# q and k turned in chunks of 128 tokens, two to a transposing DMA

## The chip, the cores and the metric

The kernel runs on one core of a Trainium2 chip. The metric is the device time of one execution in microseconds (us), the median over several runs. An engine of the core is named as in the profile: PE is TensorE (PEld its weight loads), DVE is VectorE, ACT is ScalarE, POOL is GpSimd, SP is SyncE, which computes nothing here and only issues DMAs. Each engine works through its own list of instructions in order; semaphores tie the lists together.

## What is computed

Sliding-window attention over 8 batches of 8 heads, 576 tokens and head size 64, and then a feed-forward part on the 8 x 576 = 4608 rows of 512 numbers that come out:

```
scores = (q @ k.T) / 8, kept where 0 <= row - col < 64, else -1e9
attn   = softmax(scores)              # per batch and head
x      = (attn @ v), heads side by side  -> [4608, 512]
h      = x @ w_in                     # [512, 2048]
out    = (h * cos(h)) @ w_out         # [2048, 512] -> float32 [4608, 512]
```

## The kernel before

**Blocks and groups.** A batch has NU = 9 blocks of 64 tokens. Because of the window, the queries of block j see only the keys of blocks j-1 and j, so a unit of attention is a 64 x 128 piece of scores. Four units make a group (`groups`), which goes through a chain of steps: scores on TensorE (s_ps), row maximum with mask on DVE (`g_max`), exponential and row sum on ACT (`g_exp`), reciprocal on DVE (`g_inv`), scaling to bf16 on POOL (`g_norm`, tile w), and the transpose of w into wT (`g_trans`), which for most groups is a DMA transpose issued by SP (L395). TensorE then multiplies wT by v (`values`, o_ps, L411), and DVE or ACT copies the result to xT.

**Token tiles.** The second part works on tiles of MT = 512 rows, n_mt = 9 of them. For a tile mt the loop at the end of the kernel first makes 16 blocks of h (`first` and `skewed`, h_ps, L479, 64 matmuls), lets ACT take the sine of each with a phase of pi/2 (L709) and DVE multiply (L712), and then makes the output rows (out_ps, L723, 64 matmuls, or in the last two tiles the seven products of `fast_second`). The 576 tokens of a batch don't fill whole tiles: tile mt takes the last mt blocks of batch mt - 1 and the first 8 - mt of batch mt.

**What sets the order.** Nothing is scheduled by the framework: each engine runs its instructions in the order in which the program writes them. The start (batches 0 and 1, tile 0, the loads of batch 2) is a list written out by hand, `FIRST`: `Lq2.3` in it is the load of chunk 3 of q of batch 2, `Lk2.0` of chunk 0 of k. From tile 1 on, a small planner orders the rest: `at(time, fn, ...)` puts a step down for a time, a tile being T = 32 units long, and `pump(time)`, called between pieces of the two matmul loops, writes out all steps that are due. So a step's time says between which matmuls it stands, and on SP and POOL it stands behind all that was written for them before. For batch b, t0 = T(b - 1) is the start of tile b - 1's loop, and the scores of batch b stand there as two bursts (`burst_scores`, L310), at t0 + 14.6 and t0 + 20.2 or a little later, the first with blocks 0 to 3.

**How q and k get there.** Scores need q and k with the head dimension on the partitions, that is, turned. For batches 2 to 7:

- `load_chunk` (L180): POOL issues a DMA that loads one chunk of NP = 96 tokens, all eight heads, of q or k, from float32 to bf16, into 96 partitions. Six chunks (NC) make a batch. Two buffers per name (pool `ld`).
- `turn_k` (L260): SP issues a DMA transpose per chunk into the tile kT, laid out [128, 4 pairs of heads, 576 tokens]; six per batch, written at t0 - 6 for b > 2.
- `turn_q` (L248): the same for q, into qT, for the first chunks only: `TURNED = {4: 2, 5: 2, 6: 2, 7: 6}`, so two chunks of batches 4 to 6, all six of batch 7, none of batches 2 and 3. Written at t0 - T + 23.4 (24.3 for b = 4, and 26.4 for chunks 2 to 5).
- `tr_q` with `transposed` (L223): the other chunks of q are turned by TensorE, per pair of heads one transpose a chunk into the PSUM tile tq_ps, and `put_q` lets DVE copy that to qT (L125). They stand in the loop over h of tile b - 1, at t0 + 1, 4.5, 8 and 11.5 (2, 5.3, 8.6 and 11.9 for b = 2), ahead of the first burst of the same batch.

The order that this gives SP around a tile's end is: the first four wT of a batch (t0 + 18.4 to 22.7), the turns of q of the next batch, two more wT, the turns of k of the next batch, the last wT, two stores of output (L488). `values` for tile mt is written at T mt - 1.01, so the first wT of batch mt are wanted there. `keys`, `burst_scores` and `g_scores` are the readers of qT and kT; they take 64 tokens of q and the 64 or 128 tokens of k of a unit as slices.

Of the kernel before, what the change touches and what calls it, by code (L numbers as in the profile page):

```python
# [10 lines left out]
def _safe_warn(msg, *a, **kw):  # L11
# [19 lines left out]
PAIRS = 4  # L31
# [8 lines left out]
TURNED = {4: 2, 5: 2, 6: 2, 7: 6}  # L40
# [29 lines left out]
def kernel(  # L70
# [28 lines left out]
    qsets = [const.tile([128, PAIRS, S], BF16, name=f"qT{i}") for i in range(2)]  # L99
# [76 lines left out]
    def load_chunk(name, b, c):  # L176
        if (name, b) not in st:
            st[name, b] = rows_tile(name)[0:NP].rearrange("p (c x) -> p c x", c=NC)
        src = {"q": q, "k": k}[name][b, :, c * NP:c * NP + NP]
        nc.gpsimd.dma_start(out=st[name, b][:, c].rearrange("p (h d) -> p h d", h=H),  # L180
                            in_=src.rearrange("h p d -> p h d"))
# [25 lines left out]
    def transposed(name, b, p):  # L207
# [13 lines left out]
        else:  # L221
            for c in range(TURNED.get(b, 0) if name == "q" else 0, NC):
                nc.tensor.transpose(t_ps[:, NP * c:NP * c + NP], of[:, c, 128 * p:128 * p + 128], ident[:NP, :NP])  # L223
# [3 lines left out]
    def in_order(t_ps, to, b, p):  # L227
        c = RC if b == p == 0 else NC
        return (t_ps.rearrange("d (c p) -> d p c", c=c), to.rearrange("d (p c) -> d p c", c=c)) if b < 2 else (t_ps, to)
# [4 lines left out]
    def put_q(b, p, engine=None):  # L234
        if b > 1:
            lo = TURNED.get(b, 0) * NP
            copy(engine, qsets[b % 2][:, p, lo:], st.pop(("tq", b, p))[:, lo:])
            return
        of, to = in_order(st.pop(("tq", b, p)), qsets[b][:, p], b, p)
# [7 lines left out]
    def turn_q(b, c):  # L247
        nc.sync.dma_start(out=qsets[b % 2][:, :, c * NP:c * NP + NP], in_=st["q", b][:, c], transpose=True)  # L248
# [4 lines left out]
    def k_tile(b):  # L253
        if ("kA", b) not in st:
            st["kA", b] = ka = att.tile([128, PAIRS, S], BF16, tag="kT", name="kT", bufs=2)
            st.update({("kT", b, p): ka[:, p] for p in range(PAIRS)})
        return st["kA", b]

    def turn_k(b, c):
        nc.sync.dma_start(out=k_tile(b)[:, :, c * NP:c * NP + NP], in_=st["k", b][:, c], transpose=True)  # L260

    def put_k(b, p, engine="a"):
        kt = k_tile(b)[:, p]
# [27 lines left out]
    def keys(b, p, j):  # L291
        lo, chunks = max(64 * j - 64, 0), 2 if j else 1
        rhs = st["kT", b, p][:, lo:lo + 64 * chunks].rearrange("d (a t) -> d a t", a=chunks)
# [469 lines left out]
```

## Time and profile before

| what | value |
|---|---|
| time, median of 3 runs (lowest to highest) | 303.11 us (302.81 to 303.87) |
| span of the profiled execution, first to last instruction | 301.0 us |
| busy: PE, DVE, ACT, POOL | 294.0, 234.7, 232.2, 210.3 us |
| mean granted TensorE clock | 1.000 |
| DMA packets, bytes | 159627, 41.45 MB |
| transposing DMAs issued by SP: wT, kT, qT | 60, 36, 12 |
| loads of q and k chunks issued by POOL | 36 and 36, 96 KB each |
| TensorE transposes of q, batches 2 to 6 (L223) | 96 |

The profile shows one execution, and of it the span alone; the runs' median lies 2.1 us above it. A row of a group reads: line, engine, operation, output tile <- input tiles, shape and count, then busy time and the mean of one in ns, then the idle time of the engine just before. In a table of stretches, "31.51, 31.48 (x289)" is the length of the stretch, then the busy time of the first engine in it with its number of instructions. SP's instructions are DMA issues; their duration is how long SP was held, and the landing is counted from the start of the issue to the arrival of the data.

### The profile page before, as it was taken

How to read it: one execution, taken by the hardware profiler on the slowest of the kernel's cores; microseconds unless marked ns; L12 is line 12 of the kernel's file. 1: busy time of each engine (PE TensorE's matmuls, PEld its weight loads, DVE VectorE, ACT ScalarE, POOL GpSimd, SP SyncE). 2: the span in 40 equal slices, each digit the busy share in tenths (PEclk: the TensorE clock that was granted, in tenths of full speed). 3: DMA queues.
4: the chain of work that ended last, by engine and by line, in shares of the span. 5: the costliest groups of instructions: out<-in, count | busy, mean ns of one | idle time of the engine just before them, and what ended most of it. 6: DMA issues, size and time to landing. Idle time of an engine off the chain costs nothing.

```text
span 301.0 us, 8375 instructions
## 1 busy us (share of the span) xinstructions
PE 294.0 (98%) x2863; PEld 162.5 (54%) x2863; DVE 234.7 (78%) x916; ACT 232.2 (77%) x781; POOL 210.3 (70%) x238
## 2 busy tenths in 40 slices
PE   8888999999999999999999999999999999999996
PEld 3667854644455445444454445444544454785485
DVE  4997888898887886788678876887588658985794
ACT  5997699877987699769986998699978997304610
POOL 8999568995899579995999599969997860000000
PEclk9999999999999999999999999999999999999999
DMA  7999999999999994999999999999999745003013
GB/s 146 179 206 195 198 186 138 99 154 156 219 124 112 230 119 75 115 152 188 174 108 145 165 216 115 126 152 205 134 101 119 212 86 174 2 3 139 1 37 105
DMA packets 159627, 41.45 MB, mean 138 GB/s; under 512 B 146976, under 2 KB 155232, under 8 KB 159584
## 3 DMA queue, kind: packets, MB, share of 16 engines
q0 software_dynamic: 101088, 18.06, 79.6%
q1 hardware_dynamic: 58352, 22.79, 42.3%
q8 instruction: 22, 0.36, 0.5%
q14 instruction: 21, 0.17, 0.2%
q10 hardware_dynamic: 144, 0.07, 0.1%
HBM read 36.70 MB, written 9.44 MB: 153 GB/s over the span
## 4 chain that ended last, share of the span: by engine, by line
PE 90%; DMA 4%; POOL 4%; DVE 1%; issue 0%; POOLq 0%
PE h_ps L479 37%; PE out_ps L723 28%; PE out_ps L566 8%; PE out_ps L462 5%; DMA w_in<-in_moe_w_in_dram 4%; PE h_ps L443 4%; PE s_ps L310 3%; PE o_ps L411 3%; PE tq_ps L223 1%; POOL v L186 1%; POOL q L164 1%; POOL k L164 1%; PE s_ps L332 1%; POOL w_in L202 0%; DVE xT L125 0%; PE tw_ps L392 0%
## 5 line engine op out<-in xcount | busy, mean ns | idle before, releaser
L479 PE MATMUL h_ps<-xT,w_in 128*128 128x512 bf16 x512 | 115.1, 379 | 0.2
L712 DVE TENSOR_TENSOR gT<-h_ps,sin 128x512 bf16<-128x512 f32 x128 | 85.2, 688 | 25.8 <-ACT sin L709 25.2
L709 ACT ACTIVATE sin<-h_ps 128x512 f32<-128x512 f32 x128 | 73.8, 598 | 37.0 <-PE h_ps L479 36.7
L359 ACT ACTIVATE e<-s,negm 128x128 f32<-128x128 f32 (+1 forms) x256 | 97.1, 382 | 1.7 <-POOL v L125 1.0
L723 PE MATMUL out_ps<-w_out,gT 128*128 128x512 bf16 x384 | 85.3, 379 | 0.0
L376 POOL TENSOR_TENSOR w<-e,rden 128x512 bf16<-128x512 f32 (+1 forms) x68 | 69.0, 1032 | 21.8 <-DVE rden L369 15.9
L479 PEld LDWEIGHTS <-w_in 128*128 128x128 bf16 x512 | 48.9, 98 | 54.5
L723 PEld LDWEIGHTS <-gT 128*128 128x128 bf16 x384 | 36.5, 98 | 43.1
L347 DVE CUSTOM_DVE_ANT_0 s<-s_ps,mask 128x128 f32<-128x128 f32 (+1 forms) x256 | 56.0, 277 | 1.8 <-PE s_ps L332 1.5
L359 ACT ACTIVATION_READ_ACCUMULATOR e<-s,negm 128x1 f32 x256 | 48.1, 188 | 0.0
L186 POOL DMA_DIRECT2D v<-in_v_dram x40 | 34.1, 870 | 0.1
L180 POOL DMA_DIRECT2D q<-in_q_dram x36 | 28.7, 801 | 7.7 <-DMA k<-in_k_dram 3.0
L180 POOL DMA_DIRECT2D k<-in_k_dram x36 | 28.7, 799 | 1.5 <-DVE gT L712 0.7
L369 DVE RECIPROCAL rden<-den 128x4 f32<-128x4 f32 (+1 forms) x73 | 12.2, 167 | 18.7 <-ACT e L359 18.3
L125 POOL COPY v<-v 64x1536 bf16<-64x1536 bf16 (+3 forms) x16 | 22.9, 1433 | 0.4
L347 DVE DVE_READ_ACCUMULATOR2_ANT negm<- 128x1 f32 x256 | 21.3, 83 | 0.0
L125 DVE CAST xT<-o_ps 128x512 bf16<-128x512 f32 x24 | 15.6, 679 | 4.6 <-PE o_ps L411 4.4
L443 PE MATMUL h_ps<-xT,w_in 128*128 128x256 bf16 x128 | 14.6, 273 | 0.4 <-DMA w_in<-in_moe_w_in_dram 0.4
L462 PE MATMUL out_ps<-w_out,gT 128*128 128x512 bf16 x64 | 14.8, 380 | 0.0
L443 PEld LDWEIGHTS <-w_in 128*128 128x128 bf16 x128 | 12.3, 98 | 2.1 <-DMA w_in<-in_moe_w_in_dram 0.7
L566 PEld LDWEIGHTS <-sums 128*128 128x128 bf16 x136 | 12.2, 98 | 2.0 <-DVE sums L511 0.4
L449 ACT ACTIVATE sin<-h_ps 128x512 f32<-128x512 f32 x16 | 9.3, 596 | 4.2 <-PE h_ps L443 4.2
(92 smaller groups left out, 309.4 us busy)
## 6 DMA issues: line engine op xcount, KB each, us to landing
out_dram<-out_sb SPq DMA_DIRECT2D x16, 512.0 KB, 8.3
v<-in_v_dram POOLq DMA_DIRECT2D x32, 128.0 KB, 5.6
q<-in_q_dram POOLq DMA_DIRECT2D x36, 96.0 KB, 7.3
k<-in_k_dram POOLq DMA_DIRECT2D x36, 96.0 KB, 6.1
w_in<-in_moe_w_in_dram POOLq DMA_DIRECT2D x4, 512.0 KB, 9.6
w_out<-in_moe_w_out_dram POOLq DMA_DIRECT2D x4, 512.0 KB, 11.0
q<-in_q_dram POOLq DMA_DIRECT2D x7, 144.0 KB, 5.6
k<-in_k_dram POOLq DMA_DIRECT2D x7, 144.0 KB, 5.7
```

What stands on the lines that cost most here:

```text
L125: {"a": nc.scalar.copy, "p": nc.gpsimd.tensor_copy}.get(engine, nc.vector.tensor_copy)(out, in_)
L180: nc.gpsimd.dma_start(out=st[name, b][:, c].rearrange("p (h d) -> p h d", h=H), in_=src.rearrange("h p d -> p h d"))
L186: nc.gpsimd.dma_start(out=vt.rearrange("p (h d) -> p h d", h=H), in_=v[b, :, c * 128:c * 128 + n, :].rearrange("h p d -> p h d"))
L347: nc.vector.tensor_tensor_reduce(out=s[:, u, c], in0=s_ps[:, u, c], in1=mask[:, 2 - j % 2 if j else 0, c], scale=-scale if b else -1.0, sc ...
L359: nc.scalar.activation(e[:, u, c], s[:, u, c], AF.Exp, bias=negm[:, u:u + 1], scale=1.0 if n < n_first else -1.0, accum_out=den[:, u:u + 1])
L376: (nc.gpsimd if engine == "p" else nc.vector).tensor_tensor(out=w[:, 0:u], in0=e[:, 0:u], op=ALU.mult, in1=rden[:, 0:u].unsqueeze(2).to_br ...
L443: nc.tensor.matmul(out=h_ps[:, half * e:half * e + half], lhsT=w_in_sb[:, ks, ff * 128:ff * 128 + 128], rhs=st["xT", 0][:, ks, half * g:ha ...
L479: nc.tensor.matmul(out=st["h", ff], lhsT=w_in_sb[:, ks, ff * 128:ff * 128 + 128], rhs=st["xT", mt][:, ks], start=start, stop=stop)
L566: nc.tensor.matmul(out=to[n_] if split else to[:, e], lhsT=lhs[name][f // 2][:, f % 2, 128 * e:128 * e + 128], rhs=rhs[name][:, f, lo:hi], ...
L709: nc.scalar.activation(sin, h_ps, AF.Sin, bias=math.pi / 2.0)
L712: nc.vector.tensor_tensor(out=gt[:, e], in0=h_ps, in1=sin, op=ALU.mult)
L723: nc.tensor.matmul(out=o_ps[e], lhsT=gT[ff // 2][:, ff % 2, ms * 128:ms * 128 + 128], rhs=w_out_sb[:, ff], start=ff == 0, stop=ff == n_ff - 1)
```

## The change

Chunks of q and k of batches 2 to 7 are now 128 tokens (NB = 5 to a batch, the last of 64), and `TURNS` cuts the five into (0, 1), (2, 3) and (4): one DMA transpose turns two whole chunks, the third the 64 tokens that remain. k of batches 2 to 7 and q of batches 3 to 7 are turned so, three DMA transposes each; q of batch 2 is still turned by TensorE, now in 128 columns at a time (20 transposes), with two copies per pair of heads in place of one. The tiles qT and kT change their layout from [pair, token] to [chunk, pair, token in chunk], 2560 columns instead of 2304; a double turn writes one contiguous run; batches 0 and 1 keep the old layout in the same tiles (`by_pair`), and the readers find their 64-token blocks through `blocks_of`. Where a unit's two blocks of keys lie in different chunks, the step between them is 7 blocks and not 1. All turns of q of a batch are now written at t0 - T + 23.4 (24.3 for b = 4). Of the loads, c = 4 is the last chunk of batch 3, and from batch 4 on the chunks of k that are loaded late are 3 and 4.

```diff
--- before.py
+++ after.py
@@ -37,7 +37,9 @@
 OUTS = 3
 FILL = (6, 12)
 BUSY = 8
-TURNED = {4: 2, 5: 2, 6: 2, 7: 6}
+NB = 5
+TURNS = ((0, 2), (2, 4), (4, 5))
+TURNED = (3, 4, 5, 6, 7)
 FAST = (7, 8)
 PRODUCTS = ("P1", "P2", "P6", "P5", "P7", "P3", "P4")
 
@@ -59,10 +61,10 @@
     "o.0.0.1 Pq.3.d o.1.0 Tk.3 Gs.14.3 Gs.13.0 Pk.3.d Lv0.4 Lq2.0 Ge.11 Gi.10 Gm.14 g.1.7 Lq2.1 Lq2.2 o.0.1.2 "
     "Gi.9 o.2.0 Ge.14 Gn.10.p Gm.13 Gc.10 Gi.12 o.1.1 Gs.8.3 Gs.16.4 Gm.8 o.3.0 Ge.13 o.2.1 Gi.11 oc.0.d Gn.9.p "
     "o.3.1 Gs.15.0 Gs.17.1 Gn.12.p o.0.2.3 Gi.14 Gm.15 oc.1.d Gc.9 Gn.11.p Gi.13 Gm.16 o.1.2 Ge.8 Ge.16 Ge.15 "
-    "y.1.d Gn.14.p yA.p Gi.8 Gc.12 Gm.17 o.0.3.0 Gi.16 Gn.13.p yB.p Gc.11 Gn.8.p Lq2.3 Lq2.4 Lq2.5 o.2.2 o.3.2 "
+    "y.1.d Gn.14.p yA.p Gi.8 Gc.12 Gm.17 o.0.3.0 Gi.16 Gn.13.p yB.p Gc.11 Gn.8.p Lq2.3 Lq2.4 o.2.2 o.3.2 "
     "o.1.3 Gn.16.d Gi.15 Gn.15.d Gw.8 Gc.14 Gc.13 Lk2.0 Gp.8.d Gw.16 Lk2.1 Ge.17 Lk2.2 Gp.16.d Gi.17 Lk2.3 o.2.3 "
     "oc.2.a Gw.15 Gp.15.d V.0 V.1 V.2 V.3 Gs.18.4 X.0.a X.1.d X.2.a X.3.d Gm.18 o.3.3 oc.3.d Ge.18 Gn.17.d Lk2.4 "
-    "Gi.18 Gn.18.d Lk2.5 Lv1.4 "
+    "Gi.18 Gn.18.d Lv1.4 "
 )
 
 
@@ -96,7 +98,7 @@
     ps = ctx.enter_context(tc.tile_pool(name="ps", bufs=1, space=PSUM))
     ps_t = ctx.enter_context(tc.tile_pool(name="ps_t", bufs=3, space=PSUM))
 
-    qsets = [const.tile([128, PAIRS, S], BF16, name=f"qT{i}") for i in range(2)]
+    qsets = [const.tile([128, NB * PAIRS * 128], BF16, name=f"qT{i}") for i in range(2)]
     vtiles = [const.tile([128, NU - 1, d_model], BF16, name=f"v{i}") for i in range(2)]
     w_in_sb = const.tile([128, PAIRS, d_ff], BF16, name="w_in")
     w_out_sb = const.tile([128, n_ff, d_model], BF16, name="w_out")
@@ -175,9 +177,10 @@
 
     def load_chunk(name, b, c):
         if (name, b) not in st:
-            st[name, b] = rows_tile(name)[0:NP].rearrange("p (c x) -> p c x", c=NC)
-        src = {"q": q, "k": k}[name][b, :, c * NP:c * NP + NP]
-        nc.gpsimd.dma_start(out=st[name, b][:, c].rearrange("p (h d) -> p h d", h=H),
+            st[name, b] = rows_tile(name)[:, 0:NB * d_model].rearrange("p (c x) -> p c x", c=NB)
+        n = min(128, S - 128 * c)
+        src = {"q": q, "k": k}[name][b, :, c * 128:c * 128 + n]
+        nc.gpsimd.dma_start(out=st[name, b][0:n, c].rearrange("p (h d) -> p h d", h=H),
                             in_=src.rearrange("h p d -> p h d"))
 
     def load_v(b, c):
@@ -219,24 +222,43 @@
                     nc.tensor.transpose(t_ps[64 * h:64 * h + 64, NP * c:NP * c + NP], rows[:, h, D * c:D * c + D],
                                         ident[:NP, :NP])
         else:
-            for c in range(TURNED.get(b, 0) if name == "q" else 0, NC):
-                nc.tensor.transpose(t_ps[:, NP * c:NP * c + NP], of[:, c, 128 * p:128 * p + 128], ident[:NP, :NP])
+            for c in range(NB):
+                n = min(128, S - 128 * c)
+                nc.tensor.transpose(t_ps[:, 128 * c:128 * c + n], of[0:n, c, 128 * p:128 * p + 128], ident[0:n, 0:n])
         return t_ps
 
 
     def in_order(t_ps, to, b, p):
         c = RC if b == p == 0 else NC
-        return (t_ps.rearrange("d (c p) -> d p c", c=c), to.rearrange("d (p c) -> d p c", c=c)) if b < 2 else (t_ps, to)
+        return t_ps.rearrange("d (c p) -> d p c", c=c), to.rearrange("d (p c) -> d p c", c=c)
+
+    def by_pair(x):
+        return x[:, 0:PAIRS * S].rearrange("d (h s) -> d h s", h=PAIRS)
+
+    def by_chunk(x):
+        return x.rearrange("d (c h p) -> d c h p", c=NB, h=PAIRS)
+
+    def turn(x, rows, lo, hi):
+        n = min(128, S - 128 * lo)
+        to = by_chunk(x)[:, lo:hi, :, 0:n].rearrange("d c h p -> d (c h) p")
+        nc.sync.dma_start(out=to, in_=rows[0:n, lo:hi].rearrange("p c x -> p (c x)"), transpose=True)
+
+    def blocks_of(x, b, p, lo, n):
+        if b < 2:
+            return by_pair(x)[:, p, 64 * lo:64 * lo + 64 * n].rearrange("d (a t) -> d a t", t=64)
+        at_ = [PAIRS * 2 * (i // 2) + 2 * p + i % 2 for i in range(lo, lo + n)]
+        return x.rearrange("d (a t) -> d a t", t=64)[:, at_[0]:at_[-1] + 1:at_[-1] - at_[0] or 1]
 
     def tr_q(b, p):
         st["tq", b, p] = transposed("q", b, p)
 
     def put_q(b, p, engine=None):
         if b > 1:
-            lo = TURNED.get(b, 0) * NP
-            copy(engine, qsets[b % 2][:, p, lo:], st.pop(("tq", b, p))[:, lo:])
+            t_ps, to = st.pop(("tq", b, p)), by_chunk(qsets[b % 2])[:, :, p]
+            copy(engine, to[:, 0:4], t_ps[:, 0:512].rearrange("d (c p) -> d c p", c=4))
+            copy(engine, to[:, 4, 0:64], t_ps[:, 512:S])
             return
-        of, to = in_order(st.pop(("tq", b, p)), qsets[b][:, p], b, p)
+        of, to = in_order(st.pop(("tq", b, p)), by_pair(qsets[b])[:, p], b, p)
         if b:
             copy(engine, to, of)
         elif engine == "a":
@@ -244,23 +266,22 @@
         else:
             nc.vector.tensor_scalar(to, of, scale, None, ALU.mult)
 
-    def turn_q(b, c):
-        nc.sync.dma_start(out=qsets[b % 2][:, :, c * NP:c * NP + NP], in_=st["q", b][:, c], transpose=True)
+    def turn_q(b, lo, hi):
+        turn(qsets[b % 2], st["q", b], lo, hi)
 
     def tr_k(b, p):
         st["tk", b, p] = transposed("k", b, p)
 
     def k_tile(b):
         if ("kA", b) not in st:
-            st["kA", b] = ka = att.tile([128, PAIRS, S], BF16, tag="kT", name="kT", bufs=2)
-            st.update({("kT", b, p): ka[:, p] for p in range(PAIRS)})
+            st["kA", b] = att.tile([128, NB * PAIRS * 128], BF16, tag="kT", name="kT", bufs=2)
         return st["kA", b]
 
-    def turn_k(b, c):
-        nc.sync.dma_start(out=k_tile(b)[:, :, c * NP:c * NP + NP], in_=st["k", b][:, c], transpose=True)
+    def turn_k(b, lo, hi):
+        turn(k_tile(b), st["k", b], lo, hi)
 
     def put_k(b, p, engine="a"):
-        kt = k_tile(b)[:, p]
+        kt = by_pair(k_tile(b))[:, p]
         of, to = in_order(st.pop(("tk", b, p)), kt, b, p)
         copy(engine, to, of)
 
@@ -289,8 +310,8 @@
     direct = set(range(n_first)) | {n_first + i for i in DIRECT} | set(last)
 
     def keys(b, p, j):
-        lo, chunks = max(64 * j - 64, 0), 2 if j else 1
-        rhs = st["kT", b, p][:, lo:lo + 64 * chunks].rearrange("d (a t) -> d a t", a=chunks)
+        lo, chunks = max(j - 1, 0), 2 if j else 1
+        rhs = blocks_of(st["kA", b], b, p, lo, chunks)
         return rhs[:, ::-1, :] if j and j % 2 == 0 else rhs, chunks
 
     def burst_scores(n):
@@ -308,7 +329,7 @@
                         rhs, chunks = keys(b, pe, j)
                         to = st["s", n][64 * e:64 * e + 64, u, 0:64 * chunks]
                         nc.tensor.matmul(out=to.rearrange("p (a t) -> p a t", a=chunks),
-                                         lhsT=qsets[b % 2][d, pe, 64 * j:64 * j + 64], rhs=rhs[d], start=True, stop=True,
+                                         lhsT=blocks_of(qsets[b % 2], b, pe, j, 1)[d, 0], rhs=rhs[d], start=True, stop=True,
                                          skip_group_check=True)
 
     def g_scores(n, which):
@@ -330,7 +351,7 @@
             for h in range(2):
                 d = slice(64 * h, 64 * h + 64)
                 nc.tensor.matmul(out=s_ps[d, u, 0:64 * chunks].rearrange("p (a t) -> p a t", a=chunks),
-                                 lhsT=qsets[b][d, p, 64 * j:64 * j + 64], rhs=rhs[d], start=n >= n_first,
+                                 lhsT=blocks_of(qsets[b], b, p, j, 1)[d, 0], rhs=rhs[d], start=n >= n_first,
                                  stop=n >= n_first or u == len(units) - 1, skip_group_check=True)
         st["s", n] = s_ps
 
@@ -607,25 +628,25 @@
 
     for b in range(2, B):
         t0 = T * (b - 1)
-        for c in range(TURNED.get(b, 0)):
-            at(t0 - T + (24.3 if b == 4 else 23.4 if c < 2 else 26.4) + 0.01 * c, turn_q, b, c)
-        for p in range(PAIRS if TURNED.get(b) != NC else 0):
+        for lo, hi in TURNS if b in TURNED else ():
+            at(t0 - T + (24.3 if b == 4 else 23.4) + 0.01 * lo, turn_q, b, lo, hi)
+        for p in range(0 if b in TURNED else PAIRS):
             t_q = t0 + (2 if b == 2 else 1) + (3.3 if b == 2 else 3.5) * p
             at(t_q, tr_q, b, p)
             at(t_q + 0.02, put_q, b, p)
         if b > 2:
-            for c in range(NC):
+            for c in range(NB):
                 for i, name in enumerate(("q", "k")):
-                    time = 17.9 + 2.8 * i if b == 3 and c == NC - 1 else 5.6 + 1.6 * c + 0.8 * i
-                    if b > 3 and name == "k" and c > 3:
+                    time = 17.9 + 2.8 * i if b == 3 and c == NB - 1 else 5.6 + 1.6 * c + 0.8 * i
+                    if b > 3 and name == "k" and c > 2:
                         time = (24.2 if b == 4 else 22.4) + 0.01 * c
                     if b > 4 and c == 0:
                         time = (24.26 if b == 5 else 22.46) + 0.01 * i - T
                     at(t0 - T + time, load_chunk, name, b, c)
-        for c in range(NC):
-            at(t0 + 0.1 * c - (2 if b == 2 else 6), turn_k, b, c)
+        for lo, hi in TURNS:
+            at(t0 + 0.1 * lo - (2 if b == 2 else 6), turn_k, b, lo, hi)
         for c in range(5):
-            at(t0 + (8 if TURNED.get(b) == NC else 0.5) + c, load_v, b, c)
+            at(t0 + (8 if b == B - 1 else 0.5) + c, load_v, b, c)
         for half_ in range(2):
             if b == 2:
                 at(t0 + 24.1 + 0.01 * half_, spread_v, b, half_, "p", 0, 2)
```

## The prediction

> **What bounds the kernel now.** First the page's busy shares.
>
> ```profile
> span 301.0 us, 8375 instructions
> ...
> PE 294.0 (98%) x2863; PEld 162.5 (54%) x2863; DVE 234.7 (78%) x916; ACT 232.2 (77%) x781; POOL 210.3 (70%) x238
> ```
>
> TensorE is busy 98% of the span. A busy share can flatter a pipelined engine, so the second view is the stages: I cut the span at the first h_ps matmul (L479) of each token tile mt and call the piece stage mt; this is the table of stretches for stages 1 to 6.
>
> ```profile
> core 0: us, PE busy (x) PEld busy (x) DVE busy (x) ACT busy (x) POOL busy (x), PEclk, DMA share, GB/s
> 56.97:88.77 31.80, 31.77 (x296) 15.92 (x295) 27.35 (x120) 27.12 (x100) 27.32 (x32) 1.00 1.89 166
> 88.77:120.28 31.51, 31.48 (x289) 15.60 (x288) 24.32 (x112) 27.29 (x95) 25.07 (x28) 1.00 1.22 129
> 120.28:151.45 31.17, 31.14 (x280) 15.26 (x280) 23.99 (x112) 27.08 (x95) 27.54 (x31) 1.00 1.60 157
> 151.45:182.66 31.21, 31.15 (x281) 15.27 (x280) 23.98 (x112) 27.10 (x95) 27.03 (x30) 1.00 1.61 156
> 182.66:213.83 31.17, 31.14 (x280) 15.26 (x280) 23.99 (x112) 27.03 (x95) 27.00 (x30) 1.00 1.66 155
> 213.83:244.34 30.51, 30.45 (x264) 14.57 (x264) 22.73 (x107) 27.11 (x95) 27.35 (x26) 1.00 0.92 134
> ```
>
> The columns are length, then busy time and instruction count per engine, granted clock, DMA share (over 1 because packets of two queues overlap). In every stage TensorE idles 0.03 to 0.06 us at full clock, and the next engine, ACT or POOL, has 3 us or more to spare. Stages 3 to 5 do the same work and differ from stage 6 by 16 TensorE instructions. Stage 6 is the stage whose q (batch 7) is already turned by DMA alone. The third view, the chain of work that ended last in order of time, where nearly every piece of these stages is TensorE's, says what those 16 are:
>
> ```profile
> 84.57 0.22 PE tw_ps L392 x4
> ...
> 91.52 0.26 PE tq_ps L223 x6
> ...
> 123.03 0.17 PE tq_ps L223 x4
> ...
> 166.12 0.52 PE s_ps L310 x32
> ...
> 213.83 13.97 PE h_ps L479 x64
> ```
>
> They are the transposes of q (tq_ps, L223), inserted between h_ps matmuls, four groups to a stage: six instructions and 0.26 us a group in stages 1 and 2 (batches 2 and 3), four and 0.17 us in stages 3 to 5 (batches 4 to 6). Without them 64 h_ps matmuls take 13.97 us, 218 ns each, with no hole: nothing else was waiting behind the transposes.
>
> **Weighing a rule.** The 54% of weight loads (PEld) stands in the row above. The Trainium skill, page "Perfetto Trace Analysis", section "Identifying the Most-Contended Engine", says that matmul occupancy is a poor measure of headroom and that LDWEIGHTS busy time should be used in its place; by that rule TensorE is half free and the sum below could come to nothing. The stage rows disagree here: 16 instructions fewer came with 0.66 to 0.70 us less.
>
> **The change, part by part.** *Removed from TensorE:* batch 3, 4 x 0.26 = 1.04 us (stage 2); batches 4 to 6, 4 x 0.17 = 0.68 us each (stages 3 to 5), 2.04 us. Together 3.08 us. The other way to the same number: stages 2 to 5 shrink to the 30.51 us of stage 6, which is 1.00 + 0.66 + 0.70 + 0.66 = 3.02 us. I take 3.05.
>
> *Batch 2, still on TensorE:* 24 transposes of 96 columns become 16 of 128 and 4 of 64. A group was 0.26 us; it becomes 0.22 (the four tw_ps transposes of 128, above) plus 0.03 to 0.06 for the short one, 0.25 to 0.28. Over four groups -0.04 to +0.08 us; I take 0.
>
> *DVE:* the copies of tq_ps go for batches 3 to 6, and batch 2's are split in two.
>
> ```profile
> L125 DVE COPY qT<-tq_ps 128x576 bf16<-128x576 bf16 x12 | 6.4, 544 | 0.0
> ```
>
> Batch 3's four copies are this wide, the twelve of batches 4 to 6 narrower, so 2.2 to 8.7 us less work (4 to 16 x 0.544), worth 0: in those stages DVE is busy 24 of 31 us and TensorE does not wait for it. The split adds at most 4 x 0.544 = 2.2 us in stage 1, where DVE has 4.4 us free: 0.
>
> *POOL:* 72 loads of q and k chunks become 60. A 96-token load holds POOL 0.80 us, a load of v (32 of its 40 have 128 tokens) 0.87:
>
> ```profile
> L186 POOL DMA_DIRECT2D v<-in_v_dram x40 | 34.1, 870 | 0.1
> L180 POOL DMA_DIRECT2D q<-in_q_dram x36 | 28.7, 801 | 7.7 <-DMA k<-in_k_dram 3.0 <-PE tq_ps L219 2.5 <-DVE rden L369 0.7
> ```
>
> So 72 x 0.80 = 57.6 us become 60 x 0.87 = 52 or less, off the path: 0. The bytes loaded are the same, and those issued late in a stage are still 192 tokens of k.
>
> *SP and the transposing DMAs.* Per stage SP issued 2 turns of q and 6 of k; now 3 and 3, of which two in three carry 256 tokens. The rows of the three kinds of transposing DMA, each from the view of its line (shortest, median and longest hold of SP in ns):
>
> ```profile
> L248 SPq DMA_TRANSPOSE qT<-q x12: 1185/1200/1227, 116.7 to 227.2; - x12
> ```
> ```profile
> L260 SPq DMA_TRANSPOSE kT<-k x36: 1180/1210/2237, 59.8 to 228.5; - x36
> ```
> ```profile
> L395 SPq DMA_TRANSPOSE wT<-w x60: 1188/1227/2985, 43.3 to 248.7; - x60
> ```
>
> 96 rows (q, k) and 128 rows (wT) hold SP equally long, so tokens are not what costs; a double turn has twice the columns, so its price lies between 1.2 us (one instruction) and 2.4 (two). By the near-equal rows I lean to the lower end, since a third more bytes added nothing. Three turns of q then take 3.75 to 6.2 us with their gaps, against 2.50 for two. What is queued behind them, in stage 4:
>
> ```profile
> 147.57 2.50 SPq L248 DMA_TRANSPOSE qT<-q  x2
> 151.91 3.50 SPq L395 DMA_TRANSPOSE wT<-w  x2
> 155.51 7.79 SPq L260 DMA_TRANSPOSE kT<-k  x6
> ```
>
> SP idles from 150.07 to 151.91. Turns of q that end at 151.3 move nothing; ending at 153.8 they move two wT and the turns of k by 1.9 us. The first who would feel it is TensorE's burst of scores at 166.12 (quoted above), which needs tokens 0 to 255 of k, the first three old chunks:
>
> ```profile
> L260 SPq DMA_TRANSPOSE kT<-k x1: 1207/1207/1207, 158.1 to 158.1; - x1
> ...
> DMA to landing us min/median/max: 6.4/6.4/6.4
> ```
>
> They were there at 158.1 + 6.4 = 164.5. The burst comes 0.68 us earlier in its stage, at 165.4 on this scale, so 0.9 us of cover is left. Now one double turn brings those tokens: its issue is over 1.2 to 2.4 us after 155.51 where the third old one was over after 3.8. That gives back 1.4 to 2.6 us against a loss of 0 to 1.9. I take 0. Without that cover each microsecond costs one.
>
> *A new wait:* all of q's loads must have landed before the last turn of q. The latest, in stage 5:
>
> ```profile
> L180 POOL DMA_DIRECT2D q<-in_q_dram x1: 779/779/779, 197.3 to 197.3; - x1
> ...
> DMA to landing us min/median/max: 14.1/14.1/14.1
> ```
>
> It landed at 211.4. SP's timeline there:
>
> ```profile
> 209.74 2.51 SPq L248 DMA_TRANSPOSE qT<-q  x2
> ```
>
> So the third comes to its turn at 212.2 or later: 0.8 us of cover, and fewer, larger loads ahead. Taken as 0; if it is late, the two wT behind it have a whole stage before anyone reads them, and k has the cover above.
>
> *Traffic:* q turned by DMA rises from 12 x 96 to 5 x 576 tokens of 1 KB, 1.77 MB more. On the row of the queue that SP's transfers use
>
> ```profile
> q1 hardware_dynamic: 58352, 22.79, 42.3%
> ```
>
> that is 1.77 / 22.79 x 42.3% = 3.3% of the span, an estimate by bytes: 10 us, 2.5 us in each of four stages, or 0.08 on a DMA share of 1.22 to 1.66. Stage 1 ran at 1.89 with TensorE full. Cost 0. The place where it would show is the end of a stage, where TensorE multiplies the first four wT by v. The last of them, from the SP transposes and from TensorE's timeline:
>
> ```profile
> L395 SPq DMA_TRANSPOSE wT<-w x1: 1823/1823/1823, 176.3 to 176.3; - x1
> ...
> DMA to landing us min/median/max: 4.0/4.0/4.0
> ```
> ```profile
> 181.40 1.20 PE L411 MATMUL o_ps<-wT,v 128*64 128x64 bf16 x64
> ```
>
> Landed 180.3, used 181.4: 1.1 us, of which 0.68 goes if the landing keeps its distance from the stage's start. 0.4 us is left.
>
> **Sum.** -3.08 or -3.02, taken -3.05, +0 for the rest: span 301.0 to 297.95 us. The median of the runs is 303.11, 2.1 us above the profiled span, start and end that the change does not touch; no other time of that execution is shown. 303.11 - 3.05 = **300.1 us**.
>
> **Rivals.**
>
> *Part of the gain lost at the stage ends.* The wT land later by the added traffic, say by 0.7 us of the 2.5 (the rest falls where the queues are light). Cover is 0.4 us in stage 4; I set 0.2 to 0.4 for stages 2 to 5, so 0.3 to 0.5 us of waiting in each, 1.6 in all: 301.7 us. For it: cover is thin. Against it: the turns of q come behind these wT in SP's order, and wT that waited for transfers can gain from k's turns being half as many.
>
> *Slower: double turns cost by the token.* If SP and its ring need 2.50 / 192 us per token, three turns of q last 7.5 us; in stage 4 they end at 155.1, 3.2 us after the wT should start. k lands at 164.5 + 3.2 = 167.7 against 165.4: 2.3 us of waiting. Stages 3 and 5 have more room between q's turns and the wT; I give them 0.4 us each, 3.1 us in all, which eats the gain. The stores and the last wT go 3 us deeper into the loads, the first four wT of the next batch follow late by 1 us in four stages, less 0.3 of cover: 2.8 us more, 303.1 + 2.8 = 305.9 us. It decides from 0.9 us of lateness of k; the equal 96- and 128-row prices speak against it. The landing times quoted, 4.0 us for a wT, 6.4 for k with loads under way and 14.1 for a load, speak for it: the Trainium skill, page "DMA: Bandwidth & Descriptors", section "Issuing engines are not separate DMA queues", says that transfers of all issuers interleave on the same 16 engines. The trace agrees with that.
>
> *No change.* TensorE's share misleads and another wait, ACT's or POOL's, closes in: 303.1 us. ACT's 27.1 and POOL's 27.4 us in a 30.51 us stage speak against it.
>
> **How the numbers follow.** Forecast 0.66, part lost 0.16, no change 0.08, slower 0.10. A difference under 0.3% (0.9 us) can't be told from none. Faster by more: 0.66 + 0.14 of the part-lost case = 0.80; within: 0.08 + 0.02 = 0.10; slower: 0.10. The range starts 0.5 us under the forecast (batch 2's bound, and runs that differ by 0.3 below and 0.8 above their median) and reaches over the part-lost case: 299.6 to 302.2, leaving out about 0.2.
>
> **What would show it.** Right: tq_ps of L223 only in stage 1, 20 instructions; stages 2 to 5 at 30.5 us with TensorE idle under 0.1 us in each; the turns of k over in 3.8 to 6 us. Wrong: idle time of TensorE ahead of s_ps (L310) or o_ps (L411), with k's or wT's turn landing after it; double turns that hold SP 2.4 us or more; or stages that keep 31.2 us though the 16 instructions are gone.

## The result, and the profile after

The changed kernel takes 301.61 us (median of 20 runs) against 303.51 us for the kernel before beside it; the ratio is 0.9936, 95% interval 0.9918 to 0.9955, that is 1.9 us less (1.4 to 2.5). Timed once more on another occasion the ratio was 0.9926 (0.9898 to 0.9955). The forecast was 3.05 us less, and 300.1 us; the time lies in the range (299.6 to 302.2), the size was not reached. The first lines of the page after:

```profile
span 299.7 us, 8184 instructions
...
PE 291.8 (97%) x2787; PEld 159.7 (53%) x2787; DVE 230.9 (77%) x904; ACT 232.3 (77%) x781; POOL 205.2 (68%) x226
...
q1 hardware_dynamic: 64784, 24.56, 45.7%
```

The same table of stretches as in the prediction, stages 1 to 6 of the changed kernel (length, busy time and count per engine, granted clock, DMA share):

```profile
57.39:90.00 32.61, 32.58 (x294) 16.14 (x291) 27.67 (x124) 27.24 (x100) 25.30 (x29) 1.00 1.83 169
90.00:120.47 30.47, 30.44 (x265) 14.55 (x265) 22.98 (x108) 27.20 (x95) 24.18 (x26) 1.00 1.41 147
120.47:150.94 30.47, 30.44 (x264) 14.59 (x264) 23.04 (x108) 27.08 (x95) 26.71 (x29) 1.00 1.78 177
150.94:181.57 30.63, 30.61 (x264) 14.66 (x264) 23.04 (x108) 27.22 (x96) 26.31 (x28) 1.00 1.72 164
181.57:212.05 30.48, 30.45 (x265) 14.56 (x265) 23.07 (x108) 26.91 (x95) 26.05 (x28) 1.00 1.70 177
212.05:242.56 30.51, 30.45 (x265) 14.56 (x265) 22.74 (x107) 27.11 (x95) 27.37 (x27) 1.00 1.02 126
```

Stages 2 to 5 shrank by 1.04, 0.70, 0.58 and 0.69 us, 3.01 in all: the gain came where it was forecast and in its size. Stage 1, for which the sum had 0, grew from 31.80 to 32.61, by 0.81 us. Net -2.20, inside the interval. The two profiled executions differ by 1.3 us only, because in this one stage 1 begins 0.42 us later (57.39 for 56.97) and some 0.5 us more lies behind the last matmul. The start of stage 1 lay between 56.6 and 58.7 us in the profiles below, also where nothing ahead of it was changed, so I count both as scatter.

What grew is in the chain of work that ended last, in order of time:

```profile
57.39 2.59 PE h_ps L500 x12
59.98 0.35 PE tq_ps L227 x5
...
64.25 2.70 PE h_ps L500 x12
```

Before a group of transposes, twelve h_ps matmuls take 2.59 us; behind one, 2.70. The five transposes take 0.35 us where six took 0.26. So a group costs 0.46 us against the 0.25 to 0.28 of the prediction: 0.20 us too much, four times. TensorE's own timeline around the second group shows where it goes:

```profile
63.73 0.39 PE L227 MATMUL tq_ps<-ident,q 128*128 128x128 bf16 x4
```
```profile
64.05 0.20 PE L227 MATMUL tq_ps<-ident,q 64*128 64x64 bf16 x1
64.18 0.39 PE L500 MATMUL h_ps<-xT,w_in 128*128 128x512 bf16 x1
```
```profile
64.05 0.09 PEld L227 LDWEIGHTS <-q 64*128 64x128 bf16 x1
```
```profile
64.18 0.10 PEld L500 LDWEIGHTS <-w_in 128*128 128x128 bf16 x1
```

(start, duration of the merged rows.) The four transposes of 128 rows start 0.055 us apart, the last near 63.90. The one of 64 rows starts only at 64.05, with its weight load and not after it, and the h_ps matmul behind it at 64.18, again together with its load. For the long transposes the load runs under the matmul before (the first load stands at 63.52, its transpose at 63.73). From the last long transpose to the next h_ps it is 0.28 us, where 0.055 for the long one and 0.03 for 64 columns would have been 0.085.

### The profile page after: what moved, and what is told of

Read it like the earlier page. It is cut to its first block, busy times and chain, and to the rows that moved or that the text cites. A ratio compares the mean times of both kernels' runs of the same rounds, so it can differ in the third digit from the quotient of the medians.

```text
span 299.7 us, 8184 instructions
## 1 busy us (share of the span) xinstructions
PE 291.8 (97%) x2787; PEld 159.7 (53%) x2787; DVE 230.9 (77%) x904; ACT 232.3 (77%) x781; POOL 205.2 (68%) x226
## 3 DMA queue, kind: packets, MB, share of 16 engines
q1 hardware_dynamic: 64784, 24.56, 45.7%
## 4 chain that ended last, share of the span: by engine, by line
PE 89%; DMA 6%; POOL 2%; DVE 0%; issue 0%; POOLq 0%
PE h_ps L500 37%; PE out_ps L744 28%; PE out_ps L587 8%; PE out_ps L483 5%; DMA w_in<-in_moe_w_in_dram 4%; PE h_ps L464 4%; PE o_ps L432 3%; PE s_ps L331 3%; DMA q<-in_q_dram 2%; POOL v L189 1%; PE s_ps L353 1%; PE tq_ps L227 0%; POOL w_in L205 0%; PE tw_ps L413 0%; POOL q L166 0%
## 5 line engine op out<-in xcount | busy, mean ns | idle before, releaser
L500 PE MATMUL h_ps<-xT,w_in 128*128 128x512 bf16 x512 | 112.5, 379 | 0.2
L500 PEld LDWEIGHTS <-w_in 128*128 128x128 bf16 x512 | 49.7, 98 | 58.3
L183 POOL DMA_DIRECT2D q<-in_q_dram x30 | 26.4, 883 | 4.6 <-PE tq_ps L222 2.6
L183 POOL DMA_DIRECT2D k<-in_k_dram x30 | 26.3, 886 | 0.6 <-DMA v<-in_v_dram 0.6
L464 PEld LDWEIGHTS <-w_in 128*128 128x128 bf16 x128 | 12.3, 98 | 2.3 <-DMA w_in<-in_moe_w_in_dram 1.0
```

Source lines behind the costliest of these rows:

```text
L183: nc.gpsimd.dma_start(out=st[name, b][0:n, c].rearrange("p (h d) -> p h d", h=H), in_=src.rearrange("h p d -> p h d"))
L464: nc.tensor.matmul(out=h_ps[:, half * e:half * e + half], lhsT=w_in_sb[:, ks, ff * 128:ff * 128 + 128], rhs=st["xT", 0][:, ks, half * g:ha ...
L500: nc.tensor.matmul(out=st["h", ff], lhsT=w_in_sb[:, ks, ff * 128:ff * 128 + 128], rhs=st["xT", mt][:, ks], start=start, stop=stop)
```

## Experiments

**The short transpose, taken away.** Batch 2's last chunk of q is filled up with zero rows, so that all five transposes have 128 rows.

```diff
+        if name == "q" and b == 2 and n < 128:
+            nc.vector.memset(st[name, b][n:128, c], 0.0)
...
-                nc.tensor.transpose(t_ps[:, 128 * c:128 * c + n], of[0:n, c, 128 * p:128 * p + 128], ident[0:n, 0:n])
+                nc.tensor.transpose(t_ps[:, 128 * c:128 * c + 128], of[:, c, 128 * p:128 * p + 128], ident)
```

> The changed kernel, but batch 2's last chunk of q is filled up with 64 zero rows, so that TensorE turns it as five transposes of 128 rows and none of 64 (the 64 surplus columns are not used). Theory A, the short transpose: a 64-row weight load is not overlapped with the 128-row matmul before it, nor the next 128-row load with the 64-row matmul, so a group of transposes costs 0.45 us where 0.25 to 0.28 was reckoned. Then a group is 5 x 0.056 = 0.28 us, stage 1 shrinks from 32.61 to 31.9 us, and the time is 0.7 us under the changed kernel's, a ratio to before near 0.991. Rival B, turning 128 columns at a time is dearer per column: five full transposes cost as much or more, stage 1 32.6 to 32.8. Rival C, stage 1 is longer because of something late (loads, copies out of PSUM): 32.6, unchanged.

300.39 us, ratio 0.9911 (0.9888 to 0.9934). Its chain, and its stage 1:

```profile
57.03 2.59 PE h_ps L501 x12
59.62 0.28 PE tq_ps L228 x5
...
63.64 2.59 PE h_ps L501 x12
```
```profile
57.03:88.91 31.88, 31.86 (x293) 15.99 (x291) 27.53 (x124) 27.14 (x100) 25.33 (x29) 1.00 1.76 170
```

A group is 0.28 us, the matmuls behind it are at 2.59 again, and stage 1 is 0.73 us shorter although TensorE turns more columns. That is theory A. B (dearer columns) and C (something late) fall; the two copies per pair of heads are still two here, so they are not the cause either.

**The short transpose, doubled.** One more of 64 rows in each group, between the second and the third long one.

```diff
+                if c == 1:
+                    nc.tensor.transpose(t_ps[:, 512:S], of[0:64, 4, 128 * p:128 * p + 128], ident[0:64, 0:64])
```

> The changed kernel with one more 64-row transpose in each of batch 2's four groups, put between the second and the third of 128 rows; it writes the same columns as the last one. Theory A: each passage 128 to 64 to 128 rows costs 0.28 us from start to start instead of 0.056, so 0.23 us more a group, stage 1 33.5 us. Rival B: a 64-column transpose costs 0.03 to 0.06, stage 1 32.8. Rival C: 32.6 to 32.8, hidden in the wait.

One execution. Stage 1, 32.61 with one short transpose a group, becomes

```profile
58.54:92.10 33.56, 33.54 (x296) 16.55 (x295) 27.76 (x124) 27.25 (x100) 23.67 (x27) 1.00 1.62 158
```

0.95 us more, 0.24 a group (0.23 expected). The time, 303.8 us in one run, has a start of stage 1 at 58.5 in it and is no measure of that.

**The short transpose, undone otherwise, and the changed kernel again.** Three kernels timed together: the changed one as it is, the filled-up one again, and one that loads and turns batch 2's q in six chunks of 96 tokens as before, everything else as changed.

```diff
+        if (name, b) == ("q", 2):
...
+            nc.gpsimd.dma_start(out=st[name, b][:, c].rearrange("p (h d) -> p h d", h=H),
+                                in_=q[b, :, c * NP:c * NP + NP].rearrange("h p d -> p h d"))
...
+            for c in range(NC):
+                nc.tensor.transpose(t_ps[:, NP * c:NP * c + NP], of[:, c, 128 * p:128 * p + 128], ident[:NP, :NP])
```

> The changed kernel as it is, timed beside the next two so that their ratios to the kernel before come from one chip: ratio 0.9936 as before, 301.6 us, stage 1 at 32.6 us.

> The version with batch 2's last chunk filled up to 128 rows, timed again beside the changed kernel. Theory A (the short transpose costs 0.2 us each way of a group beyond its columns): 0.7 us or so under the changed kernel, ratio 0.991, stage 1 at 31.9 us. If the first result was scatter: equal to the changed kernel, 0.9936.

> The changed kernel with one part undone: batch 2's q is loaded in six chunks of 96 tokens again and turned by TensorE in six transposes of 96 rows a group; everything else as changed. Theory A: no short transpose, a group costs 0.26 us, stage 1 at 31.8 us, ratio 0.990 to 0.991, as with the filled-up chunk. If the larger chunks of k and of later batches are what lengthens stage 1: 32.6 us still, ratio 0.9936.

| kernel | time | ratio to before (95%) | stage 1 |
|---|---|---|---|
| changed | 301.40 us | 0.9926 (0.9898 to 0.9955) | 32.61 us |
| filled up to 128 rows | 300.60 us | 0.9905 (0.9875 to 0.9935) | 31.88 us |
| batch 2's q in 96s | 300.78 us | 0.9906 (0.9868 to 0.9943) | 31.80 us |

The stages are clear; the ratios' intervals overlap, but the filled-up version came out lower on both occasions (0.9911 and 0.9905 against 0.9936 and 0.9926), by about the 0.7 us of stage 1. The 96s version keeps the larger chunks of k and of the later batches, so these do not lengthen stage 1. By the medians these two are the fastest kernels measured here.

**Batch 2's q by DMA too.**

```diff
-TURNED = (3, 4, 5, 6, 7)
+TURNED = (2, 3, 4, 5, 6, 7)
```

> The changed kernel with batch 2's q turned by DMA too (three turns ahead of k's on SP's queue); no transposes of q by TensorE are left behind batch 1. If TensorE alone bounds stage 1: four groups of 0.45 us go, stage 1 from 32.61 to 30.8 us, and the time 1.8 us under the changed kernel's, near 299.8 us, ratio to before 0.988. Rival: SP, which turns k of batch 2 from 61.4 us on, does so later behind q's turns, and TensorE waits at the first burst of scores (73.1 us, or 71.3 without the transposes): stage 1 stays at 31.5 us or more.

301.67 us, ratio 0.9948 (0.9927 to 0.9968): no better than the changed kernel. Stages 1 and 2, and TensorE's waits that it has and the changed kernel has not:

```profile
56.63:89.64 33.01, 31.08 (x272) 15.08 (x271) 25.94 (x116) 27.48 (x101) 25.62 (x29) 1.00 1.86 167
89.64:121.33 31.69, 30.98 (x264) 14.82 (x264) 22.99 (x108) 27.18 (x95) 25.05 (x27) 1.00 1.63 157
```
```profile
PE o_ps L432 <- DMA wT<-w: 2.6, 4, 1.4
```

The transposes are gone, and stage 1 is 0.4 us longer. The wait is not ahead of the burst, as the rival had it, but at the stage's end, for the first wT: one of them was 8.25 us in landing (80.28 to 88.53 in the chain). These wT were issued 2.5 us earlier than in the changed kernel (the last at 80.28, there at 82.74), and the last landed 2 us later (88.53 for 86.49): the landing is late, not the issue. Stage 1 had the highest DMA share of the changed kernel's stages, 1.83; that this traffic is what slows the landing is argued, not shown.

**The old chunks, all of q by DMA.** The kernel before with q of batches 3 to 7 turned in its own 96-token chunks, one a turn.

```diff
-TURNED = {4: 2, 5: 2, 6: 2, 7: 6}
+TURNED = {3: 6, 4: 6, 5: 6, 6: 6, 7: 6}
...
-            at(t0 - T + (24.3 if b == 4 else 23.4 if c < 2 else 26.4) + 0.01 * c, turn_q, b, c)
+            at(t0 - T + (24.3 if b == 4 else 23.4) + 0.01 * c, turn_q, b, c)
...
```

(A third line, left out here, keeps the loads of v at their times.)

> The kernel before with q of batches 3 to 7 turned by DMA alone, in its own chunks of 96 tokens, one a turn: 12 turns per stage on SP where the changed kernel has 6, the same bytes. Batch 2 as before. If SP's price is per instruction, 1.25 us each, six turns of q hold SP 7.8 us; k's third chunk then lands about when the burst wants it: stages 2 to 5 at 30.5 to 31.0 us, stage 1 at 31.8, time 300.1 to 301.5. If merging two chunks is of no use: 300.1, stages 2 to 5 at 30.5 with room. If the traffic of the turns is what hurts: stages of 31 us or more with TensorE idle ahead of s_ps.

309.9 us, ratio 1.023 (1.019 to 1.027), over every time expected. In form it is the third case, waits ahead of s_ps, though the bytes are the changed kernel's. TensorE's waits, SP's timeline around the start of stage 4, stages 3 and 4 and one stretch inside stage 4, from an execution of 312.05 us:

```profile
PE s_ps L310 <- DMA kT<-k: 5.5, 5, 1.7
PE o_ps L411 <- DMA wT<-w: 1.6, 2, 1.0
```
```profile
148.44 8.71 SPq L248 DMA_TRANSPOSE qT<-q  x6
157.23 2.53 SPq L395 DMA_TRANSPOSE wT<-w  x2
159.82 9.33 SPq L260 DMA_TRANSPOSE kT<-k  x6
```
```profile
121.36:153.00 31.64, 30.83 (x264) 14.71 (x264) 23.05 (x108) 27.37 (x95) 27.17 (x30) 1.00 1.72 163
153.00:191.03 38.03, 33.64 (x265) 15.42 (x264) 23.27 (x108) 27.49 (x95) 26.63 (x30) 0.91 1.57 140
170.80:177.60 6.80, 5.63 (x21) 2.14 (x21) 2.12 (x21) 4.18 (x24) 1.03 (x1) 0.50 1.90 143
```

The twelve turns around the start of stage 4 hold SP 18 us; k's start at 159.8, and the third of them, issued at 162.6, lands 9.4 us later, at 172, where the burst is due at 167. That is the mechanism of the "slower" rival, brought about by more instructions instead of dearer ones. And a thing that no expectation had: from that wait onward TensorE was granted half its clock for 6.8 us.

**The new chunks, one a turn.** Five turns of 128 tokens each in place of three; bytes, layout and places in the order the same.

```diff
-TURNS = ((0, 2), (2, 4), (4, 5))
+TURNS = ((0, 1), (1, 2), (2, 3), (3, 4), (4, 5))
```

> The changed kernel with its 128-token chunks turned one at a time: five DMA transposes of q and five of k per batch in place of three and three, the same bytes in the same place. If SP's price is per instruction (1.25 us, 1.3 with the gap), q's turns hold SP 2.6 us longer, the two wT and k's turns behind them start up to 2.6 us later, and k's tokens 0 to 255, now two turns, land at about 164.7 us in stage 4 where the burst wants them at 164.9: waits of 0 to 1 us ahead of s_ps in stages 3 to 5, time 301.6 to 304.5, between the changed kernel and the one with twelve turns of 96 tokens (309.9). If merging is of no use because only bytes count: 301.6, stages 2 to 5 at 30.5.

304.01 us, ratio 1.001 (0.9987 to 1.0033). Without the pairs the whole gain is gone. Stages 3 and 4 (stage 2 is 30.47), with the waits:

```profile
120.84:153.67 32.83, 30.99 (x265) 14.85 (x265) 23.06 (x108) 27.55 (x96) 29.07 (x31) 1.00 1.75 161
153.67:185.86 32.19, 32.13 (x264) 14.98 (x264) 23.05 (x108) 26.73 (x94) 23.84 (x26) 0.95 1.65 166
```
```profile
PE o_ps L432 <- DMA wT<-w: 1.8, 3, 1.0
```

The time was inside the expectation, the place was not: k was just in time (no matmul of a burst waited for it, one weight load did, for 0.4 us), and the wT at the end of stage 3 were not. Stage 4 has no wait, and yet it is 1.7 us over 30.5: its clock is 0.95, half at its beginning. This execution took 305.5 us, the longest of twelve; nine of the twelve had a mean clock of 0.999 or 1.000 where this one had 0.994. So the slow clock is this execution's. The wait in stage 3 makes that stage 2.4 us longer than the changed kernel's, which is about what the median lost; whether the other executions wait there too was not seen.

**Four chunks a turn.**

```diff
-TURNS = ((0, 2), (2, 4), (4, 5))
+TURNS = ((0, 4), (4, 5))
```

> The changed kernel with four chunks to a DMA transpose: 512 tokens and then 64, two turns of q and two of k per batch. If SP's price is per instruction, the 512-token turn holds SP 1.25 us, as the 256-token one; SP is then 2.6 us freer a stage, k of the first 256 tokens lands later by the ring time of 256 more tokens, 2 to 5 us, inside the 7 us that it has before the burst: 301.6, no change. If the price goes by columns: 2.4 us or more a turn, visible in SP's row, time still near 301.6. If a long transpose in the ring holds up the others: waits at stage ends, 302.5 or more.

301.73 us, ratio 0.9947 (0.9930 to 0.9964), the same as the changed kernel. SP's price, from the view of the turns' line, after the change (a third of its turns have 64 tokens) and here (half of them have; shortest, median and longest hold in ns):

```profile
L244 SPq DMA_TRANSPOSE kT<-k x18: 1207/1269/2759, 61.4 to 216.9; - x18
L244 SPq DMA_TRANSPOSE qT<-q x15: 1195/1251/3385, 84.1 to 209.8; - x15
```
```profile
L244 SPq DMA_TRANSPOSE kT<-k x12: 1203/1804/4136, 62.4 to 218.1; - x12
L244 SPq DMA_TRANSPOSE qT<-q x10: 1169/2030/3707, 84.0 to 211.6; - x10
```

Up to 256 tokens a turn costs one price, by the medians; at 512 it does not: the eleven 512-token turns held SP 1.85 us (at 124.7 us) to 4.14 (at 62.4), nine of them 2.4 or more. Per token most of them cost as much as the pair or more, and nothing is won. The end of stage 4 waited once for a wT, for 0.6 us.

**q of batches 3 to 6 back on TensorE.**

```diff
-TURNED = (3, 4, 5, 6, 7)
+TURNED = (7,)
```

> The changed kernel with q of batches 3 to 6 turned by TensorE as batch 2's is, five transposes a group, four of 128 rows and one of 64; q of batch 7 and all k by DMA. By the price of 0.45 us a group that stage 1 of the changed kernel shows: stages 2 to 5 grow by 1.8 us to 32.3 us, time 308.8. By the price that the prediction gave such a group, 0.25 to 0.28 us: 31.5 to 31.6 us, time near 306.

One execution, 309.72 us. Its stage 2:

```profile
91.22:123.53 32.31, 32.28 (x284) 15.83 (x284) 24.65 (x116) 27.29 (x95) 24.17 (x26) 1.00 1.10 116
```

1.84 us over the changed kernel's 30.47 there, and 0.46 us a group as in stage 1, not 0.25 to 0.28. (The time is also 0.9 us over 308.8; stage 1 began at 58.6 us here, 1.2 us later than in the changed kernel's profile.)

**The turns of q, twice.**

```diff
+        for lo, hi in TURNS if b in TURNED else ():
+            at(t0 + 0.1 * lo - 5.5, turn_q, b, lo, hi)
```

> The changed kernel with q of batches 3 to 7 turned a second time, right behind k's turns (the same data into the same place): 2.36 MB more for the transposing queue in all and three more turns of 1.3 us on SP per stage, behind q's and k's and ahead of the last wT and the stores. If the queues have room, stages 2 to 5 stay at 30.5 us and the time at 301.6. If the end of the stage is where traffic shows, the first wT of a batch land after TensorE wants them: idle time ahead of o_ps in stages 3 to 5, stages of 30.8 to 31.5 us, time 302.5 to 305.

One execution, 313.37 us, above both expectations. (The bytes of SP's queue rose from 24.56 to 27.51 MB, by 2.95 and not by 2.36: five batches, not four.) It does not tell what it was meant to. The burst of scores reads what the second turn writes and has to wait for it, and that wait is the larger part:

```profile
PE s_ps L331 <- DMA qT<-q: 5.9, 4, 2.6
PE o_ps L432 <- DMA wT<-w: 2.8, 3, 1.6
```

The 2.8 us ahead of o_ps agree with the thin cover at the stages' ends, but some of it can come from TensorE's and SP's delay, and I draw no more from it.

## Why the prediction was right, and where not

*The time and the range.* The time came out 1.5 us over the forecast. It lies inside the range because the range reached over the rival "part of the gain lost at the stage ends", whose 301.7 us it almost meets, and that is chance: the loss is not at the stage ends but in stage 1, in a term that the sum had at 0. Of the 1.5 us, 0.8 are that term and 0.4 are the base (the kernel before took 303.51 us beside the changed one, 303.11 in the sum); the 0.3 that remain are within the interval.

*Removed from TensorE, taken -3.05:* measured -3.01 in stages 2 to 5. The reading of stage 6 as the model of a stage without transposes held to 0.04 us in stages 2, 3 and 5. The doubt that the share of weight loads raised (54% before, 53% after) stays refuted here: in these stages 3 us less TensorE work was 3 us less time.

*Batch 2, taken 0, bounds -0.04 to +0.08:* this is the step that failed. It measured +0.81 us. The nearest rows gave the price of each transpose in a run of its like, and I let 64 rows cost the columns' share. What the runs showed in its place is a passage of TensorE from 128-row to 64-row operands and back, about 0.2 us beyond the columns: a group lost 0.18 us when it was taken away, gained 0.24 when it was doubled, and lost 0.20 when it was undone in another way. The Trainium skill, page "TensorEngine Tiling (Array Packing)", section "Tiling Modes", says that a change of tiling mode drains TensorE; the rows agree, with 0.13 us from the short transpose to the h_ps that follows and 0.15 to the short one from the long one before. The prediction did not weigh that rule.

The price also stood in the profile before, in rows that the prediction passed over. From one h_ps matmul to the next it is 0.218 us, and to the first 96-row transpose 0.22; but to the first s_ps matmul, on 64 x 64 operands, it is 0.31:

```profile
153.82 0.38 PE L479 MATMUL h_ps<-xT,w_in 128*128 128x512 bf16 x1
154.04 0.21 PE L223 MATMUL tq_ps<-ident,q 96*128 96x96 bf16 x1
```
```profile
165.74 0.38 PE L479 MATMUL h_ps<-xT,w_in 128*128 128x512 bf16 x1
166.05 0.22 PE L310 MATMUL s_ps<-kT,qT 64*64 64x64 bf16 x3
```

That is 0.09 us for one way. An estimate from it, 0.19 for a way there and back, would have put four groups at 0.75 us. The first o_ps matmul, with weights of 128 rows and 64 columns, also comes 0.31 us behind the out_ps before it (181.40 in the prediction's row), so what counts is not the rows alone. Rows of 96 pay nothing.

With the step right, the sum would have been 303.11 - 3.05 + 0.81 = 300.9 us. The kernels without short transposes, filled up, came out 2.9 us under the kernel before beside them both times (300.39 for 303.33, 300.60 for 303.48), near the 3.05 forecast for a batch 2 that costs nothing.

*SP's price, 1.2 to 2.4 us for a double turn, the lower end taken:* right, 1.25 and 1.27 us by the medians above. The three turns of q in stage 3's end took

```profile
145.36 4.48 SPq L244 DMA_TRANSPOSE qT<-q  x3
151.66 2.50 SPq L416 DMA_TRANSPOSE wT<-w  x2
154.26 4.40 SPq L244 DMA_TRANSPOSE kT<-k  x3
```

and moved nothing: SP sat idle from 149.8 to 151.7. Some double turns held SP longer, up to 3.4 us (the longest in the rows above), as a wT did before (2985 ns), but most did not. The price by the token, the ground of the slower rival, is out for pairs.

*k's cover, 0.9 us:* far too small, on the good side. The double turn that starts at 154.26 landed 3.7 us later, at 158.0; the chain has the burst at 164.9, and the end of that stage:

```profile
164.91 0.52 PE s_ps L331 x32
...
180.26 1.30 PE o_ps L432 x64
```

So k had 6.9 us. The estimate took the landing of the third old turn, 6.4 us behind its issue at 158.1; now one turn brings the first 256 tokens, issued at 154.3, ahead of the next loads of v (155.6). That the loads make the difference is argued.

*The stage's end, 0.4 us left:* measured, in stage 4, less than nothing. The last of the four wT was issued at 174.5 and landed 6.1 us later,

```profile
L416 SPq DMA_TRANSPOSE wT<-w x1: 1208/1208/1208, 174.5 to 174.5; - x1
...
DMA to landing us min/median/max: 6.1/6.1/6.1
```

at 180.6, 0.3 us after o_ps had begun. o_ps took 1.30 us there and 1.13 in stages 1 to 3 and 5, and stage 4 is 0.16 us longer than stage 3. The view of waits shows none, but the starts do: fifteen o_ps matmuls had started by 180.43, the next one started at 180.60, with the landing. In the second profile of the same kernel stage 4 is 30.51. The rival "part of the gain lost at the stage ends" had the right place, and in the changed kernel almost no price. In the profiles of the kernels with more turns on SP, single128 and q2_dma, the wait there is what lengthens stage 3 of the one and stage 1 of the other.

*DMA traffic:* +3.3% of the span by the estimate, 45.7 against 42.3% measured; the DMA shares of stages 2 to 5 rose by 0.04 to 0.19, 0.08 forecast. *POOL:* q and k now 26.4 + 26.3 us, 52 forecast. *DVE:* 3.8 us less, off the path, as said.

*Merging.* The prediction took the pairs as a matter of SP's time with cover on all sides. The runs say that they carry the change: five single turns instead of three, four more issues for q and k in a stage, give the whole 1.9 us back. How the longer hold of SP becomes a late landing of wT, some 20 us further on, can be read from stage 3, first of the changed kernel, then of the one with single turns:

```profile
132.54 1.20 SPq L509 DMA_DIRECT2D out_dram<-out_sb  x2
139.37 5.81 SPq L416 DMA_TRANSPOSE wT<-w  x4
```
```profile
136.93 1.09 SPq L509 DMA_DIRECT2D out_dram<-out_sb  x2
139.75 8.13 SPq L416 DMA_TRANSPOSE wT<-w  x4
```

The turns of k are over 4.5 us later with single turns, and the two stores behind them are issued 4.4 us later, though the stage begins only 0.4 us later. The second store lands at 148.1 us instead of 142.8 (10.6 and 9.6 us behind its issue at 137.6 and 133.2). From stage 1 to stage 6 all of SP's transfers landed in the order of their issue, in both traces. So the four wT that stand behind the stores, issued nearly at their old times, come in late: the first at 149.0 instead of 146.3, the last at 152.6 instead of 147.9, and TensorE idles for them from 150.4 us on.

## What to carry to other kernels

Where one engine is busy throughout, a stage that already runs without the work in question tells the gain; here each stage came out within 0.12 us of it, three of the four within 0.04. Price an instruction whose operands have another shape than its neighbours' by the passage, not by its columns, and look for a passage of that kind in the profile that you have: here filling 64 rows up with zeros made the transpose cheaper. And when work moves from a full engine to a DMA queue, count the instructions that hold the queue's issuer and look for the reader with the least cover behind them: four more issues a stage, some 5 us on SP with the same bytes, cost all that the change had saved.

## What the runs showed of the hardware that was not expected

- A 64-row transpose between 128-row work costs TensorE 0.23 to 0.24 us, where a 128-row one costs 0.055. A matmul on 64 x 64 operands, or with 128 x 64 weights, starts 0.31 us behind a 512-column one before it, where a 128 x 128 one, or one of 96 rows, starts after 0.22.
- A DMA transpose of 128 or 256 tokens by 512 columns holds SP 1.2 to 1.3 us (medians); one of 512 tokens 1.85 to 4.1 us.
- A wait of under 2 us can be followed by a loss as large. In the profiled execution of single128 TensorE waited 1.8 us between 150.4 and 152.7 us, in three pieces; then the granted clock was half for some 3.4 us:

```profile
153.67:157.20 3.53, 3.53 (x9) 1.30 (x9) 1.20 (x3) 1.63 (x2) 3.53 (x5) 0.52 1.86 196
```

  and the 64 h_ps matmuls of that stage took 15.7 us for 14.0. In single96 it was 6.8 us at half clock. In q2_dma, with 1.9 us of waiting in two pieces at the end of stage 1, the clock stayed at 1.00. In q_twice 2.3 us of waiting in two pieces, around 154 us, were followed by half clock from 155.7 to 159.1 us, and single waits of 2.6 us (to 174.6) and 2.5 us (to 207.7) were not. So the length alone does not decide; what does was not tried.
